# Loading w_in by row blocks, with six open sums for the first two tiles

## The chip, the cores and the metric

The kernel runs on one core of a Trainium2 chip. The metric is the device time of one execution in microseconds. Before the change the median of three runs is 207.99 us (207.76 to 208.26).

## The reference

Two mixers are computed from the same x (2048 rows of 512) and blended by a gate per row. Mixer A is a linear attention with softmax features over 32 heads of 16. Mixer B is a gated MLP with a product over the sequence:

```python
z = gelu(x @ w_in)                        # 512 -> 1376
z1, z2 = z[:, :688], layernorm(z[:, 688:])
g = w_sp @ z2 + b_sp[:, None]             # over the 2048 rows
b = (z1 * g) @ w_out                      # 688 -> 512
gate = sigmoid((x * gate_w).sum(-1, keepdims=True))
out = gate * a + (1 - gate) * b
```

The change touches only how `x @ w_in` and `x * gate_w` are computed for the first 256 of the 2048 rows, and how w_in is loaded.

## The kernel before

The 2048 rows are 16 tiles of 128. The contraction over 512 is cut into four blocks of 128, called dt. `w_in` is kept as four blocks of 128 rows by 1377 columns: 1376 of w_in, and gate_w as column F = 1376, so that a tile's z product also gives the logit of its gate. A tile's z takes three PSUM banks. Even tiles use banks 0 to 2 and odd tiles banks 3 to 5 (`zbank`), so tile 2 can write a bank only when the gelu has read tile 0's values there, and tile 3 follows tile 1 in the same way.

The order on each engine is written out by hand. At the start:

- Loads. The first two tiles of x are loaded as they are (L108 on SP's queue, L109 on ScalarE's). w_in follows (L112): columns 0 to 255 and 256 to 511, each as two blocks on SP and two on ScalarE's queue, then columns 512 to 1023 as two transfers on SP, then, after gate_w (L120, ScalarE's queue), columns 1024 to 1375 of all four blocks in one transfer on SP (L122). Behind that, on SP, come the transposing load of x for tiles 2 and 3 (L123), wv (L124), and the further loads of x, of the attention weights and of w_sp. The compiled program reuses eight DMA semaphores in turn, so that an SP issue can wait for the landing of the transfer eight places before it.
- TensorE. 24 products of a constant (`spin`, L189), which compute nothing that is used, then eight products that transpose x of tiles 0 and 1 (L195). VectorE copies tile 0's result into xT (L204), ScalarE tile 1's (L206). After four more spins come the z products of tiles 0 and 1 (`z_piece`, L180): for columns 0 to 255, then 256 to 511, then 512 to 1023, over the four blocks, tile 0 and tile 1 in turn.
- The gate column. gate_w is transposed by TensorE (L209), and VectorE casts it into column F of w_in (L212). The last z products of a tile are 353 columns wide and contain it.
- `z_post` takes the gelu on ScalarE (L215), the gate's tanh (L222), and the statistics of the layernorm on VectorE (L224, L227). For tile 0 parts of the gelu come earlier, as soon as a bank is complete.

Then tiles 2 to 15 run alike, twelve z products each (four of 512, four of 512, four of 353 columns), and from tile 5 on with the v projection of an older tile (L282) and the folding of the attention weights (L305) between them. The stages behind (features, the product with w_sp at L405, the attention, the output) aren't touched.

Of the kernel before, what the change touches and what calls it, by code (L numbers as in the profile page):

```python
# [19 lines left out]
F = 1376  # L20
FH = 688
HF = FH // 2
NT = S // P
NDT = D // P
CH = 512
# [14 lines left out]
def kernel(  # L40
# [14 lines left out]
    nc = tc.nc  # L55
# [11 lines left out]
    def zbank(t):  # L67
        b = 3 * (t % 2)
        return ps[:, b:b + 3, :].rearrange("p b n -> p (b n)")

    xT = pers.tile([P, NDT, S], BF16, name="xT")
    w_in = pers.tile([P, NDT, F + 1], BF16, name="w_in")
# [30 lines left out]
        out=ident[:], in_=ident[:], pattern=[[-1, P]],  # L103
# [3 lines left out]
    w_in_v = B_w_in.rearrange("(dt p) f -> p dt f", p=P)  # L107
    nc.sync.dma_start(out=xn[:, 0, :], in_=x2[0:P, :])  # L108
    nc.scalar.dma_start(out=xn[:, 1, :], in_=x2[P:2 * P, :])  # L109

    def load_w_in(eng, d0, d1, n0, n1):
        eng.dma_start(out=w_in[:, d0:d1, n0:n1], in_=w_in_v[:, d0:d1, n0:n1])  # L112

    HC = CH // 2
    for n0 in (0, HC):
        load_w_in(nc.sync, 0, 2, n0, n0 + HC)
        load_w_in(nc.scalar, 2, 4, n0, n0 + HC)
    for d0 in (0, 2):
        load_w_in(nc.sync, d0, d0 + 2, CH, 2 * CH)
    nc.scalar.dma_start(out=gw[:], in_=gate_w.rearrange("(dt p) -> dt p", p=P))  # L120
    nc.scalar.activation(out=st[:, 9, 0:1], in_=ones[:, 0:1], func=AF.Gelu_apprx_tanh)
    nc.sync.dma_start(out=w_in[:, :, 2 * CH:F], in_=w_in_v[:, :, 2 * CH:F])  # L122
    nc.sync.dma_start_transpose(out=xT[:, :, 2 * P:CH], in_=x2[2 * P:CH, :])  # L123
    nc.sync.dma_start(  # L124
        out=wv[:, :, :],
        in_=A_wqkv[:, 2 * D:3 * D].rearrange("(dt p) n -> p dt n", p=P),
    )
    for q in range(1, NCH):
        nc.sync.dma_start_transpose(
            out=xT[:, :, q * CH:(q + 1) * CH], in_=x2[q * CH:(q + 1) * CH, :]  # L130
        )
        if q == 1:
            nc.sync.dma_start(
                out=wphiW[:, :, :],
                in_=A_w_phi.rearrange("(g h) e f -> (h e) g f", g=NDT),
# [3 lines left out]
        out=bcolb[:, :, :], in_=B_b_sp.rearrange("(t p) -> t p", p=P)  # L139
# [7 lines left out]
    for t in range(WSLOTS):  # L147
        load_wsp(t)
    nc.sync.dma_start(
        out=w_out[:, 0:NFT - 1, :],  # L150
        in_=B_w_out[0:(NFT - 1) * P, :].rearrange("(ft p) n -> p ft n", p=P),
# [4 lines left out]
        out=w_out[0:last_m, NFT - 1, :], in_=B_w_out[(NFT - 1) * P:FH, :]  # L156
    )
    nc.sync.dma_start(
        out=wo[:, :, :], in_=A_wo.rearrange("(g p) n -> p g n", p=P)
# [4 lines left out]
        out=mask16[:], in_=mask16[:], pattern=[[-16, 8]],  # L164
# [3 lines left out]
        out=mask16[:], in_=mask16[:], pattern=[[16, 8]],  # L168
# [8 lines left out]
    def z_piece(t, n0, n1, d0=0, d1=NDT):  # L177
        zb = zbank(t)
        for dt in range(d0, d1):
            nc.tensor.matmul(  # L180
                zb[:, n0:n1], lhsT=xT[:, dt, t * P:(t + 1) * P], rhs=w_in[:, dt, n0:n1],
                start=(dt == 0), stop=(dt == NDT - 1),
            )

    Z_PIECES = [(0, CH), (CH, 2 * CH), (2 * CH, F + 1)]

    def spin(n):
        for _ in range(n):
            nc.tensor.matmul(  # L189
                ps[:, 5, 0:P], lhsT=ones, rhs=ones, start=True, stop=True  # L190
            )

    def x_transpose(t):
        for dt in range(NDT):
            nc.tensor.matmul(  # L195
                ps[:, 6 + t, dt * P:(dt + 1) * P], lhsT=xn[:, t, dt * P:(dt + 1) * P],
                rhs=ident[:], start=True, stop=True,
            )
# [9 lines left out]
    def gate_column():  # L208
        nc.tensor.matmul(  # L209
            ps[:, 6, 0:NDT], lhsT=gw[:], rhs=ident[0:NDT, 0:NDT], start=True, stop=True  # L210
        )
        nc.vector.tensor_copy(out=w_in[:, :, F], in_=ps[:, 6, 0:NDT])  # L212

    def z_gelu(t, n0, n1):
        nc.scalar.activation(  # L215
            out=zz[:, t, n0:n1], in_=zbank(t)[:, n0:n1], func=AF.Gelu_apprx_tanh
        )

    def z_post(t, done=0):
        zb = zbank(t)  # L220
        z_gelu(t, done, F)
        nc.scalar.activation(out=gth[:, t:t + 1], in_=zb[:, F:F + 1], func=AF.Tanh, scale=0.5)  # L222
        for h in range(2):
            nc.vector.bn_stats(  # L224
                out=stats[:, t, h, :], in_=zz[:, t, FH + h * HF:FH + (h + 1) * HF]
            )
        nc.vector.bn_aggr(out=mv[:, t, :], in_=stats[:, t, :, :].rearrange("p h s -> p (h s)"))  # L227
# [241 lines left out]
    oTpool = ctx.enter_context(tc.tile_pool(name="oTp", bufs=LAG + 2))  # L469

    VLAG = 5
    spin(24)
    x_transpose(0)
    x_transpose(1)
    for d0, d1 in ((0, 1), (1, 2), (2, NDT)):
        x_copy(0, d0, d1)
        x_copy(1, d0, d1)
    spin(4)
    for n0, n1 in ((0, HC), (HC, CH), Z_PIECES[1]):
        for dt in range(NDT):  # L480
            z_piece(0, n0, n1, dt, dt + 1)
            z_piece(1, n0, n1, dt, dt + 1)
        if n1 == CH:
            z_gelu(0, 0, CH)
            gate_column()
    z_gelu(0, *Z_PIECES[1])
    z_piece(0, *Z_PIECES[2])
    z_post(0, done=2 * CH)
    z_piece(1, *Z_PIECES[2])
    z_post(1)  # L490
    build_wphi()
    for t in range(2, NT):
# [96 lines left out]
```

## Time and profile before

| What | us |
|---|---|
| median of three runs | 207.99 |
| the profiled execution | 208.12 |
| its span, first to last instruction | 206.4 |
| TensorE busy | 202.3 |
| VectorE busy | 148.5 |
| ScalarE busy | 82.1 |
| z products (L180), 200 of them | 39.7 |
| product with w_sp (L405), 512 of them | 84.1 |

The busy time of TensorE counts overlapping matmuls once, and an instruction's own duration is longer than the distance to the next one, since they are pipelined. A price per matmul is therefore read from the distance of starts, or from the chain, which lays the pieces end to end. What the DMA queues bring in the first microseconds, by the page:

```profile
w_in<-in_B_w_in_dram SPq DMA_DIRECT2D x2, 256.0 KB, 4.5
...
w_in<-in_B_w_in_dram SPq DMA_DIRECT2D x1, 352.0 KB, 4.9
w_in<-in_B_w_in_dram ACTq DMA_DIRECT2D x2, 128.0 KB, 4.0
w_in<-in_B_w_in_dram SPq DMA_DIRECT2D x2, 128.0 KB, 3.6
```

The columns are the destination and source, the queue, the number of transfers, the size of each (in KiB), and the median time from issue to landing.

### The profile page before, as it was taken

How to read it: one execution, taken by the hardware profiler on the slowest of the kernel's cores; microseconds unless marked ns; L12 is line 12 of the kernel's file. 1: busy time of each engine (PE TensorE's matmuls, PEld its weight loads, DVE VectorE, ACT ScalarE, POOL GpSimd, SP SyncE). 2: the span in 40 equal slices, each digit the busy share in tenths (PEclk: the TensorE clock that was granted, in tenths of full speed). 3: DMA queues.
4: the chain of work that ended last, by engine and by line, in shares of the span. 5: the costliest groups of instructions: out<-in, count | busy, mean ns of one | idle time of the engine just before them, and what ended most of it. 6: DMA issues, size and time to landing. Idle time of an engine off the chain costs nothing.

```text
span 206.4 us, 3685 instructions
## 1 busy us (share of the span) xinstructions
PE 202.3 (98%) x1399; PEld 117.8 (57%) x1399; DVE 148.5 (72%) x304; ACT 82.1 (40%) x145; POOL 49.5 (24%) x46
## 2 busy tenths in 40 slices
PE   8999999999999999999999999999999999999994
PEld 8545555554455666666666667666455555555542
DVE  1049858385887888879898996798989788796500
ACT  4266767675684324250505102222524243341122
POOL 4000000000002353525352543032532252322000
PEclk9999999999999999999999999999999999999999
DMA  5999899997000638463757781145756974566451
GB/s 160 289 178 247 189 170 226 168 192 231 0 3 0 140 65 117 102 112 85 153 126 109 139 174 41 38 91 84 161 131 122 127 176 98 129 141 153 110 110 51
DMA packets 90378, 26.50 MB, mean 128 GB/s; under 512 B 84296, under 2 KB 90360, under 8 KB 90360
## 3 DMA queue, kind: packets, MB, share of 16 engines
q1 hardware_dynamic: 87360, 23.87, 60.2%
q10 hardware_dynamic: 3000, 2.39, 3.8%
q8 instruction: 11, 0.18, 0.4%
q14 instruction: 7, 0.06, 0.1%
HBM read 3.44 MB, written 2.10 MB: 27 GB/s over the span
## 4 chain that ended last, share of the span: by engine, by line
PE 96%; DMA 2%; SPq 0%; ACT 0%; issue 0%
PE ps L405 36%; PE ps L180 18%; PE ps L326 13%; PE ps L448 10%; PE ps L453 7%; PE ps L282 7%; DMA w_in<-in_B_w_in_dram 2%; PE ps L427 2%; PE ps L377 2%; PE ps L305 1%; SPq L112 0%; SPq L108 0%; ACT ob L457 0%; PE ps L209 0%
## 5 line engine op out<-in xcount | busy, mean ns | idle before, releaser
L405 PE MATMUL ps<-zz,wsp 128*128 128x344 bf16 x512 | 84.1, 309 | 0.0
L343 POOL TENSOR_TENSOR w_in<-w_in,rs 128x512 bf16<-128x512 bf16 x28 | 41.3, 1475 | 124.7 <-DVE rs L341 112.4
L405 PEld LDWEIGHTS <-wsp 128*128 128x128 bf16 x512 | 49.9, 98 | 28.1
L334 ACT ACTIVATE w_in<-ps 128x512 bf16<-128x512 f32 x56 | 30.1, 596 | 63.3 <-issue 21.4
L180 PE MATMUL ps<-w_in,xT 128*128 128x512 bf16 (+2 forms) x200 | 39.7, 350 | 0.4 <-DMA w_in<-in_B_w_in_dram 0.4
L339 DVE TENSOR_REDUCE zs<-w_in 128x64 f32<-128x1024 bf16 x28 | 33.8, 1209 | 0.0
L413 DVE SCALAR_TENSOR_TENSOR u<-ps,bcol,zz 128x344 bf16<-128x344 f32 x32 | 18.4, 574 | 18.6 <-PE ps L427 8.3
L180 PEld LDWEIGHTS <-xT 128*128 128x128 bf16 x200 | 19.1, 98 | 18.0 <-issue 0.8
L215 ACT ACTIVATE zz<-ps 128x1376 bf16<-128x1376 f32 (+2 forms) x18 | 21.4, 1190 | 18.6 <-PE ps L180 18.6
L448 PE MATMUL ps<-w_out,uT 128*128 128x512 bf16 (+2 forms) x102 | 23.5, 366 | 0.0
L224 DVE BATCH_NORM_STATS2 stats<-zz 128x6 f32<-128x344 bf16 x32 | 14.8, 505 | 11.1 <-ACT zz L215 11.1
L377 PE MATMUL ps<-vv,w_in 128*128 128x65 bf16 x128 | 21.7, 193 | 0.0
L343 DVE TENSOR_TENSOR w_in<-w_in,rs 128x512 bf16<-128x512 bf16 x28 | 19.4, 693 | 1.0
L341 DVE RECIPROCAL rs<-zs 128x64 f32<-128x64 f32 x32 | 17.7, 553 | 3.2
L457 ACT ACTIVATE ob<-ps 128x512 bf16<-128x512 f32 (+2 forms) x17 | 9.7, 572 | 25.1 <-PE ps L453 19.9
L453 PE MATMUL ps<-wo,oT 128*128 128x512 bf16 (+2 forms) x68 | 16.6, 366 | 0.0
L326 PEld LDWEIGHTS <-xT 128*128 128x128 bf16 x128 | 10.8, 98 | 9.9
L326 PE MATMUL ps<-wq,xT 128*128 128x512 bf16 x64 | 16.4, 379 | 0.0
L326 PE MATMUL ps<-wk,xT 128*128 128x512 bf16 x64 | 16.3, 379 | 0.0
L427 PE MATMUL ps<-kvx,wqkT 128*128 128x68 bf16 x128 | 15.8, 194 | 0.0
L282 PE MATMUL ps<-wv,xT 128*128 128x512 bf16 x64 | 15.6, 379 | 0.0
L448 PEld LDWEIGHTS <-uT 128*128 128x128 bf16 x102 | 9.5, 98 | 10.4
(56 smaller groups left out, 134.3 us busy)
## 6 DMA issues: line engine op xcount, KB each, us to landing
out_dram<-ob ACTq DMA_DIRECT2D x15, 128.0 KB, 2.1
w_out<-in_B_w_out_dram SPq DMA_DIRECT2D x1, 640.0 KB, 4.9
w_in<-in_B_w_in_dram SPq DMA_DIRECT2D x2, 256.0 KB, 4.5
wv<-in_A_wqkv_dram SPq DMA_DIRECT2D x1, 512.0 KB, 5.0
wo<-in_A_wo_dram SPq DMA_DIRECT2D x1, 512.0 KB, 5.3
w_in<-in_B_w_in_dram SPq DMA_DIRECT2D x1, 352.0 KB, 4.9
w_in<-in_B_w_in_dram ACTq DMA_DIRECT2D x2, 128.0 KB, 4.0
w_in<-in_B_w_in_dram SPq DMA_DIRECT2D x2, 128.0 KB, 3.6
```

The lines of the kernel that those rows point to most:

```text
L180: nc.tensor.matmul(zb[:, n0:n1], lhsT=xT[:, dt, t * P:(t + 1) * P], rhs=w_in[:, dt, n0:n1], start=(dt == 0), stop=(dt == NDT - 1),)
L215: nc.scalar.activation(out=zz[:, t, n0:n1], in_=zbank(t)[:, n0:n1], func=AF.Gelu_apprx_tanh)
L282: nc.tensor.matmul(ps[:, b, :], lhsT=xT[:, dt, t * P:(t + 1) * P], rhs=wv[:, dt, :], start=(dt == 0), stop=(dt == NDT - 1),)
L326: nc.tensor.matmul(ps[:, b, :], lhsT=xT[:, dt, t * P:(t + 1) * P], rhs=w[:, dt, :], start=(dt == 0), stop=(dt == NDT - 1),)
L334: nc.scalar.activation(out=e[:, :, a, :], in_=src, func=AF.Exp, scale=sc)
L339: nc.vector.tensor_reduce(out=zs[:], in_=ev, axis=AX.X, op=ALU.add)
L343: eng.tensor_tensor(out=ev[:, sl, :], in0=ev[:, sl, :], in1=rs[:, sl, None].to_broadcast([P, H, DH]), op=ALU.mult,)
L377: nc.tensor.matmul(slots[:, g, 0:HW + 1], lhsT=ek_t[t][:, g, :, :].rearrange("p a n -> p (a n)"), rhs=vv[:, t, g, 0:HW + 1], start=(t == 0 ...
L405: nc.tensor.matmul(ps[:, b, 0:HF], lhsT=wsp[:, tt % WSLOTS, s, :], rhs=zz[:, s, FH + h * HF:FH + (h + 1) * HF], start=(s == 0), stop=(s == ...
L427: nc.tensor.matmul(slots[:, g, 0:QW], lhsT=eT_t[t][:, g, :], rhs=kvx[:, g, :], start=True, stop=True)
L448: nc.tensor.matmul(ps[:, b, n0:n1], lhsT=uT[:, ft, :], rhs=w_out[:, ft, n0:n1], start=(ft == 0), stop=False,)
L453: nc.tensor.matmul(ps[:, b, n0:n1], lhsT=oT[:, g, :], rhs=wo[:, g, n0:n1], start=False, stop=(g == NDT - 1),)
```

## The change

w_in is loaded by blocks of its rows, all 1376 columns at once. Blocks 0 and 1 are each cut in two halves of 688 columns, one on SP's queue and one on ScalarE's; blocks 2 and 3 are one transfer each on SP. There are six transfers of w_in where there were seven.

The z products of tiles 0 and 1 go over dt on the outside: each block feeds six products (512, 512 and 352 columns for each tile) into six sums that stay open in six banks. The column of the gate is taken out of them. Its transpose by TensorE comes after the second block, and eight products of one column follow the last block. All gelus of the two tiles come after them in program order. There are three more spins at the start. Tiles 2 to 15 are as before.

```diff
-    def load_w_in(eng, d0, d1, n0, n1):
-        eng.dma_start(out=w_in[:, d0:d1, n0:n1], in_=w_in_v[:, d0:d1, n0:n1])
-
-    HC = CH // 2
-    for n0 in (0, HC):
-        load_w_in(nc.sync, 0, 2, n0, n0 + HC)
-        load_w_in(nc.scalar, 2, 4, n0, n0 + HC)
-    for d0 in (0, 2):
-        load_w_in(nc.sync, d0, d0 + 2, CH, 2 * CH)
+    def load_w_in(eng, dt, n0, n1):
+        eng.dma_start(out=w_in[:, dt, n0:n1], in_=w_in_v[:, dt, n0:n1])
+
+    for dt in (0, 1):
+        load_w_in(nc.sync, dt, 0, FH)
+        load_w_in(nc.scalar, dt, FH, F)
     nc.scalar.dma_start(out=gw[:], in_=gate_w.rearrange("(dt p) -> dt p", p=P))
     nc.scalar.activation(out=st[:, 9, 0:1], in_=ones[:, 0:1], func=AF.Gelu_apprx_tanh)
-    nc.sync.dma_start(out=w_in[:, :, 2 * CH:F], in_=w_in_v[:, :, 2 * CH:F])
+    for dt in (2, 3):
+        load_w_in(nc.sync, dt, 0, F)
...
-    spin(24)
+    spin(27)
...
-    for n0, n1 in ((0, HC), (HC, CH), Z_PIECES[1]):
-        for dt in range(NDT):
-            z_piece(0, n0, n1, dt, dt + 1)
-            z_piece(1, n0, n1, dt, dt + 1)
-        if n1 == CH:
-            z_gelu(0, 0, CH)
+    FIRST = [(0, CH), (CH, 2 * CH), (2 * CH, F)]
+    for dt in range(NDT):
+        for t in (0, 1):
+            for n0, n1 in FIRST:
+                z_piece(t, n0, n1, dt, dt + 1)
+        if dt == 1:
             gate_column()
-    z_gelu(0, *Z_PIECES[1])
-    z_piece(0, *Z_PIECES[2])
+    for t in (0, 1):
+        z_piece(t, F, F + 1)
+    z_gelu(0, *FIRST[0])
+    z_gelu(0, *FIRST[1])
     z_post(0, done=2 * CH)
-    z_piece(1, *Z_PIECES[2])
     z_post(1)
```

## The prediction

> **What bounds the kernel now.** I read the page's busy shares first, then the chain that ended last, then the first 24 us engine by engine, then the DMA rate stretch by stretch.
>
> ```profile
> PE 202.3 (98%) x1399; PEld 117.8 (57%) x1399; DVE 148.5 (72%) x304; ACT 82.1 (40%) x145; POOL 49.5 (24%) x46
> ...
> PE 96%; DMA 2%; SPq 0%; ACT 0%; issue 0%
> ```
>
> TensorE is busy 98% of the span and is 96% of the chain. So the end moves only if TensorE's work changes or its idle time does. The 2% of DMA in the chain is the one stretch that this edit touches.
>
> ```profile
> 0.83 2.72 PE L189 MATMUL ps<-const-bfloat16-1.0 128*128 128x128 bf16 x24 [0.83 <-PEq L573]
> ...
> 3.38 1.03 PE L195 MATMUL ps<-ident,xn 128*128 128x128 bf16 x8
> ...
> 4.64 1.15 PE L180 MATMUL ps<-w_in,xT 128*128 128x256 bf16 x8
> 6.22 1.05 PE L180 MATMUL ps<-w_in,xT 128*128 128x256 bf16 x8 [0.43 <-DMA w_in<-in_B_w_in_dram]
> ...
> 7.21 0.17 PE L209 MATMUL ps<-ident,gw 4*128 4x4 bf16 x1
> ...
> 7.31 12.57 PE L180 MATMUL ps<-w_in,xT 128*128 128x512 bf16 x64
> ...
> 8.96 0.18 DVE L212 CAST w_in<-ps 128x4 bf16<-128x4 f32 x1 [4.12 <-DMA w_in<-in_B_w_in_dram]
> ...
> 19.72 1.03 PE L282 MATMUL ps<-wv,xT 128*128 128x512 bf16 x4
> ```
>
> The reader should see three things: TensorE waits at 6.22 for the second w_in pieces; the cast of the gate column waits for the last w_in piece and comes at 8.96; and from 7.31 on L180 runs as one block up to 19.72. No wait of TensorE is listed behind 6.22, so whatever the first two tiles gain or lose reaches the end unchanged.
>
> Unit prices come from the chain of the same stretch:
>
> ```profile
> 19.88 0.86 PE ps L282 x4
> 20.75 0.22 PE ps L305 x4
> 20.97 2.33 PE ps L180 x12
> ```
>
> A 512-wide product takes 0.86/4 = 0.216 us, a 128-wide one 0.22/4 = 0.056, and a tile of twelve z products 2.33, which leaves (2.33 - 8 x 0.216)/4 = 0.15 for a 353-wide one. The spins at the start are 128 wide too but stand 0.107 apart (2.72 us for 24), so TensorE runs at half speed there, though the page's clock row prints a full grant; by the starts of the first z products, 0.21 and then 0.11 apart, full speed comes at 4.86. Tile 2 starts four tiles before 19.72: 19.72 - 4 x 2.33 = 10.39. This is the mark to compare.
>
> **The change, part by part** (profiled execution: 208.12 us, a span of 206.4 and 1.7 around it; it lies 0.13 over the median 207.99).
>
> Spins, three added: 3 x 0.107 = 0.32. Before, TensorE stood 0.04 for x to land (3.34), and that goes, so transposes and first z product come 0.28 to 0.31 later: the first z product at 4.95 instead of 4.64. The casts of xT on VectorE and ScalarE move along by 0.31; tile 1's first is then written by about 5.05 and its first product comes at 4.95 + 0.58 = 5.53, so they stay hidden.
>
> z products: 32 become 24 wide ones, the same columns; two tiles cost 2 x 2.33 = 4.66. The 256-wide ones stand 0.109 apart, so halving cost nothing before either.
>
> Gate column's transpose (L209), moved behind the second block: before, it stretched the step from a 256-wide product to the next one from 0.11 to 0.31, so 0.20, and I keep that. Its weights gw lie behind the ACT queue's w_in pieces in both kernels and are wanted at 4.95 + 2.33 = 7.28, about when they are now.
>
> Gate column's products, eight added, one column wide, each with its own 128x128 weights. The trace has no one-column product. Low end: the 68-wide L427 starts 0.03 before its successor, 8 x 0.03 = 0.24. High end: the isolated 4-wide L209 at 0.20, 8 x 0.20 = 1.6. These eight have the weights' shape and no change of shape between, like L427, so I take 0.24 and keep 1.6 as a rival. The 353rd column that they replace is worth 0.4 ns each.
>
> The wait of the cast L212 moves off the path: it is released by the last block and is wanted only at 9.8. Behind it on VectorE stand tile 0's statistics, which follow tile 0's last gelu (about 10.6) and so don't meet it. Before, it cost the step from 512 to 353 wide: 7.31 to 10.39 is 3.08 for 8 x 0.216 + 8 x 0.15 = 2.93, so 0.15.
>
> Sum without a DMA wait: 4.95 + 4.66 + 0.20 + 0.24 = 10.05 for tile 2, 0.34 earlier than 10.39.
>
> Loads. Starts plus time to landing give for the pieces now: 128 KiB each at 4.06 (SP) and 4.34 (ACT), 6.18 (SP) and 6.64 (ACT), then 256 KiB at 7.02 and 7.83, and the last 352 KiB at 8.88. The new blocks are 344 KiB (352 kB) each, with rows of 1376 or 2752 bytes for 512, 1024 and 704. The rates:
>
> ```profile
> 3.50:4.50 1.00, 1.00 (x12) 1.00 (x11) 0.47 (x3) 0.95 (x3) 0.00 (x0) 1.00 0.96 230
> 4.50:5.50 1.00, 1.00 (x11) 0.82 (x9) 0.35 (x2) 0.68 (x3) 0.00 (x0) 1.00 0.90 258
> ...
> 6.50:7.50 1.00, 1.00 (x9) 0.62 (x8) 0.00 (x0) 0.30 (x1) 0.00 (x0) 1.00 1.09 354
> ```
>
> The last column is GB/s: 230 and 258 while the 512-byte rows go, 354 with the longer rows, at much the same busy share of the DMA engines. Early end: 90 kB more than the first pair (4.34) and then 352 kB each at 354 GB/s: 4.6, 5.6, 6.6, 7.6. Late end, today's landings by bytes: 5.13, 6.90, 7.85, 8.88. TensorE wants them at 4.95 (ACT's half 0.22 later), 6.11 (6.33), 7.47 and 8.63. At the early end nothing waits; at the late end only the second block does. Rows are 2.7 to 5.4 times those that were slow, so I stand near the early end and put 0.1 us on the second block.
>
> The Trainium skill ("DMA: Bandwidth & Descriptors", Specifications) says that transfers of 512 B and up already reach line rate, so longer rows would bring nothing; by that rule the late end holds. The trace disagrees so far, 230 against 354 GB/s.
>
> ScalarE: all gelus of the first two tiles now come behind the last block. Tile 0's first can start at 9.05 (its last product begins at 8.63 and takes 0.38), then 0.6, 0.6, 0.46, 0.17 and tile 1's 1.32: done by 12.2 at the latest. Tile 3, which wants tile 1's banks, starts at 10.05 + 2.33 = 12.38. The cover is 0.18 us; if it goes, tile 3 waits by what is missing.
>
> SP: one issue of 0.47 less in front, so the x transpose for tiles 2 and 3 is issued about 0.5 earlier. It landed at 9.85 (4.47 + 5.4), 0.96 behind the last w_in piece; it may not land later than 10.05, which holds even at the late end. The later loads on SP come earlier too.
>
> **Total:** 208.12 - 0.34 + 0.1 = 207.88 for this execution, 207.75 against the median. The 0.1 is the softest term; I forecast 207.7. A measurement here tells a change from none at about 0.2%, 0.42 us; 207.7 is inside.
>
> **The rivals.**
> (a) *Clock opens early.* The old kernel's tile 2 hangs on landings (last one 8.88, cast 9.14, then 8 x 0.15), so it doesn't care when full speed comes; the new one does. With full speed from the transposes on, their 12 matmuls take 0.67 for 1.28, but the first block lands at 4.6, so tile 2 starts at 9.70, 0.69 earlier: 207.3. For it: nothing else would bind. Against: this profile shows 4.86.
> (b) *Clock opens late*, 1 us: the first products run at half speed, 0.5 back: 10.55, so 0.16 later: 208.15.
> The Trainium skill ("TensorE: Matmul & The Clock Gate", Part 1) puts the opening some 4 us into sustained activity, give or take 0.5. The trace agrees, 4.86 - 0.83 = 4.03; that other executions differ isn't shown here.
> (c) *Row blocks land as bytes do today.* The second block's second half at 6.90 instead of 6.33 costs 0.57: 10.62, 208.2; if both halves land together the loss is 0.79: 10.84, 208.4. For it: the ACT pieces always landed 0.27 to 0.46 behind SP's. Against: the rates above.
> (d) *The slower side: one-column products cost what the isolated L209 does.* Tile 2 at 4.95 + 4.66 + 0.20 + 1.6 = 11.41, so 1.02 later: 209.0. It turns slower from 0.24/8 + 0.34/8 = 0.07 us each, and beyond 0.2% from 0.125. For it: eight sums into two columns, the weights changed each time. Against: L427 and L377 at 0.03.
>
> **Chances.** Forecast 0.42, (a) 0.24, (b) 0.07, (c) 0.17, (d) 0.10. The forecast gives 0.08 of its part to faster, as 207.57 is close; (a) is faster; (c) is split 0.08 within and 0.09 beyond (208.41), (b) 0.05 and 0.02, (d) 0.01 and 0.09. Faster 0.32, within 0.34 + 0.08 + 0.05 + 0.01 = 0.48, slower 0.20. Low end of the range: (a) with another 0.1, 207.2. High end: (c) in its worse form with 0.1, 208.5. Left out are (d) and the edge of (a) and (b).
>
> **What would show it.** First L180 product at 4.95; no wait of TensorE within the 24, or one short one at 6.1 to 6.3; L212's cast about 8 with nobody behind it; eight narrow L178 products within 0.3 us; tile 2 at 10.0 to 10.2; full use of TensorE after that. Wrong: a long wait for w_in inside the 24 (c), a stretch above 0.6 us for the narrow products (d), first products 0.43 apart (b), a wait of tile 3 for ScalarE, or of tile 2 for the x transpose.

## The result, and the profile after

The changed kernel takes 208.66 us (median of 19 runs, 207.80 to 209.52) against 207.97 (19 runs, 207.67 to 208.36) on the same chip: a ratio of 1.0034, 95% interval 1.0021 to 1.0047. It is slower, by 0.7 us, and its single runs lie 1.7 us apart where those of the old kernel lie 0.7 apart. The profiled execution took 208.91, a span of 207.2.

The page of the changed kernel, the lines that answer to the first ones shown before:

```profile
PE 202.5 (98%) x1402; PEld 117.7 (57%) x1402; DVE 148.6 (72%) x304; ACT 81.9 (40%) x145; POOL 49.5 (24%) x46
...
PE 95%; DMA 3%; ACTq 0%; ACT 0%; issue 0%
```

TensorE's busy time is 0.2 us more, while the span is 0.8 longer: TensorE stands longer, and the chain puts it down to DMA, 3% where it was 2%. The timeline of the first microseconds tells where:

```profile
0.84 3.04 PE L187 MATMUL ps<-const-bfloat16-1.0 128*128 128x128 bf16 x27 [0.84 <-PEq L572]
...
4.95 1.55 PE L178 MATMUL ps<-w_in,xT 128*128 128x512 bf16 x7
...
7.43 1.12 PE L178 MATMUL ps<-w_in,xT 128*128 128x512 bf16 x5 [0.93 <-DMA w_in<-in_B_w_in_dram]
...
8.48 0.17 PE L207 MATMUL ps<-ident,gw 4*128 4x4 bf16 x1
...
8.59 8.69 PE L178 MATMUL ps<-w_in,xT 128*128 128x512 bf16 x50
8.69 0.18 DVE L210 CAST w_in<-ps 128x4 bf16<-128x4 f32 x1 [3.53 <-PE ps L207]
10.19 1.50 ACT L213 ACTIVATE zz<-ps 128x512 bf16<-128x512 f32 x3 [4.70 <-PE ps L178]
```

Seven products run from 4.95: the six of block 0 and the first of block 1. The eighth needs the columns of block 1 that ScalarE's queue loads, and starts at 7.43. The seventh started at 6.13, so the step that should take 0.22 took 1.31: a loss of 1.09 us (the 0.93 in brackets counts from the modelled end of the seventh). Behind it TensorE runs without a stop. The landing of the two halves of block 1, from the view of the tile w_in in the stretch in which they are issued (SP's and ScalarE's at 1.72 and 1.73; shortest, median and longest time to landing):

```profile
DMA to landing us min/median/max: 4.2/4.9/5.7
```

SP's half lands at 5.93, ScalarE's at 7.39. They were issued together and are the same size. Block 2 (7.58) and block 3 (8.45) are then in time.

```profile
20.64 0.86 PE ps L280 x4
```

This row of the chain answers to the one at 19.88 before. All is later by 0.76, so tile 2 starts at 10.39 + 0.76 = 11.15.

The rate at which the data came (us; then busy time of TensorE, weight loads, VectorE, ScalarE, GpSimd; granted clock, DMA share, GB/s):

```profile
3.50:4.50 1.00, 1.00 (x12) 1.00 (x11) 0.16 (x1) 0.81 (x2) 0.00 (x0) 1.00 1.11 376
4.50:5.50 1.00, 1.00 (x10) 0.76 (x8) 0.66 (x3) 0.72 (x3) 0.00 (x0) 1.00 0.99 331
5.50:6.50 1.00, 1.00 (x6) 0.39 (x4) 0.00 (x0) 0.00 (x0) 0.00 (x0) 1.00 1.03 407
6.50:7.50 1.00, 0.07 (x2) 0.07 (x1) 0.00 (x0) 0.00 (x0) 0.00 (x0) 1.00 1.93 213
```

331 to 407 GB/s from 3.5 to 6.5, where the old kernel had 230 to 312 in the trace of the prediction (275 to 336 in a second one, below). The bytes came faster than in the first, and yet ScalarE's half of block 1, wanted at 6.34, landed at 7.39, only 0.19 before block 2.

The trace's DMA records, one for each row (a contiguous piece of a transfer, which goes to one partition), suggest how. They don't name the DMA engine, so what follows is put together from their times. In the trace the semaphore of such a transfer is counted up 16 times. For ScalarE's half of block 1, 14 of the 16 counts are there by 5.43, the 15th at 5.94 and the last, which is the landing, at 7.39. So most of the 16 DMA engines were done early, and one was behind: two rows took 0.73 and 0.42 us, where a row of 1376 bytes takes 0.059. When that engine came to ScalarE's half, SP's queue had block 2 waiting on it, and the rows alternated:

```
ScalarE's queue, rows of 1376 B, start: 6.22  6.38  6.55  6.72  6.88 us; the end mark (4 bytes) 7.04
step: 0.16 to 0.17 us = 0.059 (its row) + 0.109 (a row of 2752 B of block 2 on SP's queue)
```

After the end mark at 7.04 comes the last count at 7.39. So, as far as the times tell, one DMA engine of 16 set the landing.

### The profile page after: what moved, and what is told of

It reads as the page before. It is cut to its first block, busy times and chain, and to the rows that moved or that the text cites. A ratio compares the mean times of both kernels' runs of the same rounds, so it can differ in the third digit from the quotient of the medians.

```text
span 207.2 us, 3688 instructions
## 1 busy us (share of the span) xinstructions
PE 202.5 (98%) x1402; PEld 117.7 (57%) x1402; DVE 148.6 (72%) x304; ACT 81.9 (40%) x145; POOL 49.5 (24%) x46
## 4 chain that ended last, share of the span: by engine, by line
PE 95%; DMA 3%; ACTq 0%; ACT 0%; issue 0%
PE ps L403 36%; PE ps L178 18%; PE ps L324 13%; PE ps L446 10%; PE ps L451 7%; PE ps L280 7%; DMA w_in<-in_B_w_in_dram 3%; PE ps L425 2%; PE ps L375 2%; PE ps L303 1%; ACTq L112 0%; ACTq L109 0%; ACT ob L455 0%; PE ps L207 0%
## 5 line engine op out<-in xcount | busy, mean ns | idle before, releaser
L178 PE MATMUL ps<-w_in,xT 128*128 128x512 bf16 (+3 forms) x200 | 39.7, 349 | 0.9 <-DMA w_in<-in_B_w_in_dram 0.9
L178 PEld LDWEIGHTS <-xT 128*128 128x128 bf16 x200 | 18.5, 98 | 18.9 <-issue 1.2
L324 PEld LDWEIGHTS <-xT 128*128 128x128 bf16 x128 | 10.8, 98 | 9.9
```

The source lines that it names most:

```text
L178: nc.tensor.matmul(zb[:, n0:n1], lhsT=xT[:, dt, t * P:(t + 1) * P], rhs=w_in[:, dt, n0:n1], start=(dt == 0), stop=(dt == NDT - 1),)
L324: nc.tensor.matmul(ps[:, b, :], lhsT=xT[:, dt, t * P:(t + 1) * P], rhs=w[:, dt, :], start=(dt == 0), stop=(dt == NDT - 1),)
```

## The experiments

Theory A: ScalarE's half of block 1 is late because of the long rows of block 2 that alternate with it. Theory B: block 1 would be late in any queue. A third theory, C, came out of the first four traces. Ratios are to the old kernel, run on the same chip; the chip isn't the same for all experiments.

**Block 1 in one transfer on SP, behind its half of block 0.**

```diff
-    for dt in (0, 1):
-        load_w_in(nc.sync, dt, 0, FH)
-        load_w_in(nc.scalar, dt, FH, F)
+    load_w_in(nc.sync, 0, 0, FH)
+    load_w_in(nc.scalar, 0, FH, F)
+    load_w_in(nc.sync, 1, 0, F)
```

> Block 1 goes as one transfer on SP's queue; ScalarE's queue keeps x, half of block 0 and gate_w. In the changed kernel the only wait inside the 24 z products is for ScalarE's half of block 1, landing at 7.39; SP's half landed at 5.93. Theory A (the half is late because on a DMA engine that fell behind its rows alternate with SP's rows of block 2, twice as long): in one queue block 1 can't be overtaken by block 2, lands at about 6.0 to 6.5, the wait shrinks from 1.1 us to at most 0.2, tile 2 starts at 10.05 to 10.3 instead of 11.15, and the time falls by 0.8 to 1.0 us to 207.6 to 207.9. Theory B (the bytes or a stalled DMA engine make block 1 late in whatever queue it is): block 1 lands at 6.9 or later, a wait of 0.6 to 1.1 us stays, 208.3 to 208.7.

208.54 against 207.78, 1.0033 (1.0020 to 1.0045). Block 1 landed at 6.78, between what the two theories had put. Nothing of the loss went away: as put, theory A is wrong. Putting block 1 in front of block 2 in one queue doesn't help as long as its own rows are long. The wait in this trace was only 0.2 us, though, as A had put and B had not; another 0.48 went to a cause that neither theory had (theory C below).

**Block 2 in two halves of columns.**

```diff
-    for dt in (2, 3):
-        load_w_in(nc.sync, dt, 0, F)
+    load_w_in(nc.sync, 2, 0, FH)
+    load_w_in(nc.sync, 2, FH, F)
+    load_w_in(nc.sync, 3, 0, F)
```

> Block 2 goes on SP's queue as two halves of 688 columns, so that the rows that alternate with ScalarE's half of block 1 are 1376 bytes long instead of 2752. Theory A: on an engine that is behind, a pair of rows takes 2 x 0.059 = 0.12 us instead of 0.16, over 8 pairs 0.35 us less; the half of block 1 lands about 0.35 earlier and the time is about 208.3 (half of the gap to the kernel with block 1 on SP at most). Theory B: row length of what runs beside it doesn't matter, 208.6 to 208.8.

207.70 against 207.78, 1.0002 (0.9988 to 1.0016). Block 1 landed at 5.50 and 5.68 and TensorE didn't wait. That is more than A had expected.

**Only the gate column moved, the old loads kept.**

```diff
-    z_piece(0, *Z_PIECES[2])
-    z_post(0, done=2 * CH)
-    z_piece(1, *Z_PIECES[2])
+    for t in (0, 1):
+        z_piece(t, 2 * CH, F)
+    for t in (0, 1):
+        z_piece(t, F, F + 1)
+    z_post(0, done=2 * CH)
```

> The old kernel with its old loads; only the gate column is taken out of the 353-wide products of tiles 0 and 1 and put behind them as eight products of one column. Theory A: this part is worth -0.15 (the wait for the cast goes) and +0.2 (8 x 0.025), though the last w_in piece's landing at 8.88 still bounds the 352-wide products: between -0.1 and +0.1 us, 207.9 to 208.1. A rival that puts the loss of the changed kernel into the narrow products or the later gelus expects 208.4 or more.

208.10, 1.0012 (0.9998 to 1.0026), not told from no change. The expectation was put against 207.99; the old kernel took 207.78 on this chip, so the rival's loss of 0.4 us would be a ratio of 1.0020, inside the interval: this run doesn't rule it out. The trace of the changed kernel does, in which eight narrow products take 0.20 us and tile 3 doesn't wait for the gelus. In the trace of this run the 352-wide products start at 9.34, 0.57 after the last piece of w_in had landed (8.77), so there the loads didn't set the start of tile 2.

**24 spins in the changed kernel** (`spin(27)` back to `spin(24)`).

> The changed kernel with 24 spins instead of 27. Theory A and B: the first z product comes 0.28 us earlier, but the wait for block 1 takes it back, so no change against the changed kernel, 208.5 to 208.8. Rival (the three spins are what the change lost): 0.3 us less, 208.35, with the wait for block 1 no longer than before.

207.96, 1.0013 (0.9997 to 1.0029). Neither theory had this: with the loads of the changed kernel, more than half of the loss was gone by the medians, though the interval reaches into that of the changed kernel. Its trace has block 1 at 5.86 and 6.04 and no wait, with block 2 in long rows: they don't delay block 1 in every execution. An earlier start of the z products explains 0.3 us at most; the rest stays unexplained.

These traces brought up something that the page doesn't show. The trace's clock record, which begins when TensorE gets its full speed, begins at another time in each: 4.86 (old kernel), 4.97 (changed), 5.92, 4.78, 6.60 and 4.81 us. The page prints a full clock from the start of the span in all of them. Theory C: the changed kernel, bound by TensorE from 4.95 on, pays half of every microsecond by which full speed is late; the old one spends that time waiting for loads. It was put to the test with the next four.

**The changed kernel unaltered, beside three variants.**

> The changed kernel, unaltered, beside three variants on one chip, for the comparisons and for a second trace. Theory A (queue): again a wait of about 1 us for the second block, and 208.6. Theory C (new: full speed of TensorE comes at another time in each execution; it came at 4.86, 4.97, 5.92, 4.78, 6.60 and 4.81 us in the six traces so far, and the changed kernel, which is bound by TensorE from 4.95 on, loses half of what it comes later, while the old one waits for loads in that time): the median is the same 208.5 to 208.7, but the second trace shows less wait where full speed came later, and the tile-2 start is 10.05 plus half of (full speed - 4.95) plus any wait.

208.98 against 207.94, 1.0052 (1.0031 to 1.0073). The timeline of this second trace of the changed kernel:

```profile
4.72 1.32 PE L178 MATMUL ps<-w_in,xT 128*128 128x512 bf16 x6
6.51 0.38 PE L178 MATMUL ps<-w_in,xT 128*128 128x512 bf16 x1 [0.47 <-DMA w_in<-in_B_w_in_dram]
7.74 1.12 PE L178 MATMUL ps<-w_in,xT 128*128 128x512 bf16 x4 [0.85 <-DMA w_in<-in_B_w_in_dram]
```

Full speed came early here (4.43), and TensorE waited for both halves of block 1, landing at 6.47 and 7.70. ScalarE's half ended on rows 0.16 us apart again.

**Block 2 in halves, again, and with 24 spins.**

> Block 2 in two halves on SP's queue, again, now beside the changed kernel on the same chip. Theory A: 0.4 us or more below the changed kernel (the first time 207.70 against 207.78 for the old one). Theory C alone: the row length of block 2 does nothing, the same as the changed kernel within 0.2 us, and the first result was the chip or luck.

> Block 2 in two halves and 24 spins. Theory A: at most 0.3 us below the kernel with 27 spins, as the second block still lands at 5.7 to 6.0 and is wanted at 5.8. Theory C: the z products start 0.3 us earlier, and half-speed products are done while TensorE would be spinning, so 0.15 to 0.3 us below the one with 27 spins whatever the loads do. Both: about 207.4, which would be under the old kernel.

208.03, 1.0004 (0.9993 to 1.0014), and 207.71, 0.9995 (0.9983 to 1.0006). So on one chip the short rows take 0.95 us off the changed kernel, with intervals that don't overlap, and bring it to the old one. The three spins are worth 0.3 us by the medians, within the intervals.

**36 spins in place of 4 in front of the z products.**

```diff
-    spin(4)
+    spin(36)
```

> The changed kernel with 36 spins instead of 4 between the copies of xT and the z products, so that every block has landed before it is wanted and only TensorE's speed sets the start of tile 2. Theory C: the time is 209.2 to 209.4 when full speed comes at 4.87 and half a microsecond more for each microsecond later, so the single runs spread over more than 1 us, up to 210.8, with a median about 210. A and B, with full speed always near 4.9: all runs within 0.3 us of 209.3.

209.87, 1.0089 (1.0072 to 1.0107), runs from 209.26 to 210.30. TensorE has no wait for a load in its trace:

```profile
4.53 2.83 PE L187 MATMUL ps<-const-bfloat16-1.0 128*128 128x128 bf16 x36
7.19 2.50 PE L178 MATMUL ps<-w_in,xT 128*128 128x512 bf16 x11
9.62 0.17 PE L207 MATMUL ps<-ident,gw 4*128 4x4 bf16 x1
```

The 36 spins start at 4.53 and end at 7.19, 0.074 each on average, between 0.107 and 0.056, so full speed came in the middle: their starts fall from 0.107 to 0.058 apart at about 5.74 (this trace has no clock record). The five runs spread over 1.04 us, though no load is waited for; but the 26 runs of the old kernel on this chip spread over 1.06, so the spread alone doesn't single out the clock. The median, 209.87, is 0.5 to 0.7 above the 209.2 to 209.4 of full speed at 4.87 and near the 210 that theory C had put; A and B had put 209.3. Theory C holds here, and the starts of the spins show the change of speed directly. The trace also gives the pure price of the stretch: from the first z product to tile 2, 12.28 - 7.19 = 5.09 us at full speed (four blocks, the transpose and the narrow products).

**A control for the short rows: two transfers for block 2, cut by partitions.**

```diff
+    for p0 in (0, P // 2):
+        nc.sync.dma_start(
+            out=w_in[p0:p0 + P // 2, 2, 0:F], in_=w_in_v[p0:p0 + P // 2, 2, 0:F]
+        )
```

> A control for the short rows of block 2: block 2 again in two transfers on SP, issued at the same times as the two column halves, but cut by partitions, so that its rows keep 2752 bytes. Theory A (row length of what alternates with ScalarE's half of block 1): as the changed kernel, block 1 complete at 7.2 to 7.7, ratio to the old kernel 1.003 to 1.005. Rival D (two smaller transfers, the second issued 1.1 us later, let block 1 through): as with short rows, block 1 complete at 5.7 to 6.6, ratio 1.000 to 1.0005.

208.55, 1.0030 (1.0021 to 1.0038): as the changed kernel. Same number of transfers, same order, long rows, and the loss is back. The two halves of block 1 landed at 6.57 and 6.75 in its trace, later than with short rows (5.50 and 5.68; 5.95 and 6.60) and earlier than I had put. So by the run times the rows of block 2 decide, not the number of transfers or when they are issued. The trace doesn't show the path, as TensorE waits for no load in it:

```profile
4.95 3.23 PE L181 MATMUL ps<-w_in,xT 128*128 128x512 bf16 x12
```

What this execution lost, it lost to a late full speed (6.42).

**One queue, short rows** (block 1 on SP in two column halves, block 2 too).

> Block 1 on SP's queue in two halves of 688 columns, block 2 too. With block 1 as one transfer of long rows on SP it landed at 6.78 and the ratio was 1.0033. If short rows as such make block 1 land in time: 6.0 to 6.4 and a ratio of 1.000 to 1.001. If what counts is that two queues feed the DMA engines at once (a stalled packet of one leaves the engine to the other): block 1 complete at 6.6 or later, ratio 1.002 or more, as with long rows.

207.98, 1.0000 (0.9989 to 1.0011), block 1 complete at 5.81. One queue does as well as two, if the rows are short. In its trace TensorE waits for no load, and yet:

```profile
4.95 3.34 PE L180 MATMUL ps<-w_in,xT 128*128 128x512 bf16 x12
8.22 0.17 PE L209 MATMUL ps<-ident,gw 4*128 4x4 bf16 x1
```

Twelve products and the step to the transpose take 8.22 - 4.95 = 3.27, where full speed needs 2 x 1.16 + 0.1 = 2.42. The 0.85 more is half of the 1.69 by which full speed (6.64) came after the first product. This kernel's runs fall in two groups, 207.54 to 207.79 and 208.17 to 208.56.

**One queue, block 1 short, block 2 long.**

> Block 1 on SP in two halves of short rows, block 2 behind it on the same queue in one transfer of long rows. Theory A (the harm is the alternation with the other queue): block 2's rows can't get between block 1's, so block 1 is complete by 5.8 to 6.4, as with short rows everywhere, ratio 0.999 to 1.001. Rival E (long rows anywhere among the first three blocks slow the DMA engines down): block 1 or block 2 late by 0.5 us or more, ratio 1.002 to 1.005.

208.39, 1.0016 (1.0002 to 1.0029), between the two expectations; its interval touches both that of the changed kernel and that of short rows everywhere. In its trace, where full speed came early (3.53), block 1 landed at 6.29 and 6.74 and cost 0.77 and 0.24 us by the distances of starts. So long rows behind a short block in the same queue, where nothing can alternate with another queue, may cost something too. But with short rows everywhere (the next run) block 1 landed at 6.19 and 6.66, hardly earlier. This stays open.

**Attempts at a faster kernel.**

> Block 1 and block 2 in short rows on SP, 24 spins instead of 27. If TensorE bounds the stretch, as theory C says where the loads are in time: 0.15 to 0.3 us under the one with 27 spins (ratio 1.000), so 0.9987 to 0.9993. If the landings bound it: 1.000.

207.82, 0.9995 (0.9985 to 1.0006). In its trace the first z product starts at 4.40, which takes full speed for the last spins, and TensorE then waited for block 1 (6.19 and 6.66): when the clock is early the landings bound the stretch.

> An attempt to beat both kernels: short rows for block 2, 24 spins, gate_w loaded by GpSimd's queue and transposed by TensorE before the z products, in place of two spins. The transpose's 0.2 us leave the stretch that TensorE bounds: against the kernel with short rows and 24 spins (ratio 0.9995) 0.2 us less, a ratio of 0.9985 if TensorE bounds the stretch; unchanged if the landings or the clock do.

208.60, 1.0042 (1.0022 to 1.0062), with runs up to 210.4. gate_w landed at 5.26 and TensorE stood for it, here in the trace (the 0.58 counts from a modelled end):

```profile
5.30 0.18 PE L209 MATMUL ps<-ident,gw 4*128 4x4 bf16 x1 [0.58 <-DMA gw<-in_gate_w_dram]
5.42 7.74 PE L180 MATMUL ps<-w_in,xT 128*128 128x512 bf16 x34
```

In that execution (210.4 us) full speed came at 10.04 only. ScalarE's half of block 1 landed at 7.28, although block 2 went in short rows; at half speed TensorE didn't wait for it.

> Short rows for block 2, 24 spins, and gate_w on ScalarE's queue between its halves of blocks 0 and 1, with TensorE's transpose of it in place of two spins in front of the z products. gate_w should land by 4.5, so that TensorE doesn't stand as it did with GpSimd's load (5.26). If TensorE bounds the stretch: 0.2 us under the kernel with 24 spins (ratio 0.9995), so 0.998 to 0.999. If gate_w lands later than 4.6, or the landings of block 1 bound the stretch: no gain or a loss, 0.9995 or more.

207.91, 1.0004 (0.9988 to 1.0020): no gain.

```profile
4.99 0.16 PE L209 MATMUL ps<-ident,gw 4*128 4x4 bf16 x1 [0.39 <-DVE xT L204]
5.09 7.20 PE L180 MATMUL ps<-w_in,xT 128*128 128x512 bf16 x41
```

This time gate_w isn't what TensorE stands for: the transpose writes the bank from which VectorE is still copying xT. What was saved later was lost here.

**The old kernel once more.**

> The old kernel, for another trace. Theory C: wherever full speed comes between 4.4 and about 6.5, tile 2 starts at 10.3 to 10.6, since the last w_in piece (8.9) and the cast bound it.

One run, 207.85. Full speed came at 5.51, 0.65 later than in its first trace, and tile 2 started at 10.15, 0.24 earlier, as the last piece of w_in landed at 8.65 instead of 8.88. It follows the landing (1.51 behind it in both traces), not the clock, but the 10.3 to 10.6 were too narrow. How far this goes is seen above, in the run with the gate column moved: with full speed at 6.60 its products, in the order of the old kernel up to there, came later than the landing.

## Why the prediction was wrong

The forecast was 207.7, within 0.2% of the old kernel, with a range of 207.2 to 208.5; the time is 208.66, above it. By its steps:

- Spins: right. The first z product was put at 4.95 and came at 4.95; in the other traces with 27 spins and this order it came between 4.39 and 4.96, early where full speed was early.
- Wide products, transpose and narrow products: right. 4.66 + 0.20 + 0.24 were 5.10; without a wait it is 5.09. The narrow products start 0.025 us apart in the trace, so rival (d) is out.
- The cast L210 holds nobody up, the gelus don't hold up tile 3, and the x transpose lands at 9.98, before tile 2 wants it: as put, though 0.13 later than before and not earlier. Tile 2 at the forecast 10.05 would have had 0.07 of cover.
- Loads: this is the term that failed. I put "0.1 us on the second block"; it cost 1.09 in the first trace and 1.64 in the second (both halves late). The step that failed is "Rows are 2.7 to 5.4 times those that were slow, so I stand near the early end". I took the rate for the landing. Even my late end, 6.90, the landing by bytes of rival (c), lay below the 7.39 and 7.70 measured; that rival had the wait in the right place, at 0.57 to 0.79 us. By the run times the rows that I counted as a gain were what cost: with rows of 1376 bytes for block 2 the ratio is 1.0002 and 1.0004, with 2752 bytes 1.0034, 1.0052 and, in two transfers, 1.0030, all with 27 spins. In one queue: 1.0033 with both blocks long, 1.0016 with block 2 long, 1.0000 with both short.
- The rates, on which that step stood, didn't show what I read in them. Of the 258 kB that moved from 4.5 to 5.5 in the old kernel, 163 were in rows of 1024 bytes already; its second trace has 275 and 336 GB/s where the first has 230 and 258; and the kernel with block 1 whole on SP has 239 and 250 there, with rows of 1376 and 2752 bytes. So 230 against 354 GB/s was no measure of the row length. I also overlooked that at the late end the first block, 5.13 against 4.95, would have waited too; it doesn't change that sum, as the second block's landing sets it.
- The clock: rivals (a) and (b) had the mechanism, and "it doesn't care when full speed comes; the new one does" is what was found. The sum, though, took the 4.86 of one trace as the rule, and I gave the early side 0.24 and the late side 0.07. With short rows no wait is left, the sum without a wait says -0.34, and the kernel measures as the old one: by the traces the clock takes most of the difference. It cost 0.65 and 0.85 in the traces where it came at 6.25 and 6.64, and 0.23 on average over the eight traces with 27 spins and the changed kernel's order (first z product against 4.95, plus the half-speed loss).

The Trainium skill ("TensorE: Matmul & The Clock Gate", Part 1) has the opening some 4 us into sustained activity, give or take 0.5. The first trace agreed; of all 14 traces that have a clock record and kept TensorE busy up to it, 7 agree and 7 don't: counted from TensorE's first product at 0.83 or 0.84, it took from 2.7 (one queue, block 2 long) to 5.8 us (one queue, short rows).

How far the two terms carry, trace by trace (us): first z product + 5.09 + half of what full speed came later + waits for loads, against the start of tile 2 that the trace has.

| kernel | first z | full speed | half-speed loss | waits | sum | tile 2 |
|---|---|---|---|---|---|---|
| changed | 4.95 | 4.97 | 0.01 | 1.09 | 11.14 | 11.15 |
| changed, second trace | 4.72 | 4.43 | 0 | 1.64 | 11.45 | 11.46 |
| block 1 long on SP | 4.96 | 5.92 | 0.48 | 0.2 | 10.73 | 10.76 |
| block 2 short | 4.88 | 4.78 | 0 | 0 | 9.97 | 9.98 |
| block 2 short, again | 4.95 | 6.25 | 0.65 | 0 | 10.69 | 10.70 |
| block 2 long, two transfers | 4.95 | 6.42 | 0.74 | 0 | 10.78 | 10.78 |
| one queue, short | 4.95 | 6.64 | 0.85 | 0 | 10.89 | 10.89 |

The two work against each other in one execution: when full speed comes late, TensorE reaches block 1 later and waits less (0.2 in the third row) or finds it landed (the sixth row has long rows and no wait). That two things can each delay a run would explain why the runs of the changed kernel scatter more than those of the old one, where tile 2 follows the last landing in both traces; no run tests this by itself.

What is shown: that the wait for block 1 is the loss in both traces of the changed kernel; that with 27 spins the row length of block 2 decides the run times (the control with two long transfers); and that the clock moves this stretch by itself (the spins in front of the z products, and the table). Seen in the traces of the changed kernel only, and not proved by an experiment of its own: that the harm comes by rows alternating on an engine that is behind. The landings of single traces don't settle it. With block 1 on two queues it was complete between 6.04 and 7.70 in five traces with block 2 in long rows, and between 5.68 and 7.28 in five with short ones. The two outliers, 6.04 (24 spins) and 7.28 (gate_w on GpSimd's queue), are from kernels with another change besides. The run with block 2 long in one queue falls between, and why 24 spins with long rows lost so little stays open.

No version was found that is faster than the old kernel beyond the uncertainty; the best two, both at 0.9995, aren't told from it.

## What to carry to other kernels

A block that others wait for lands when the last of its DMA engines is done with it (here the last of 16 counts came 1.45 us behind the 15th): judge a load by its landing and by what shares its engines, not by the rate. Here shorter rows for what was queued behind it were worth 0.95 us on one chip; by which path is open, so try it rather than count on it. Before a start-up stretch is moved from being bound by loads to being bound by TensorE, ask when full speed comes; if that varies between executions, the old waits were hiding it, and one profile can't price it.

## What had not been expected of the hardware

- Full speed of TensorE came between 3.53 and 6.64 us in nine traces with the same 27 spins from 0.84 on (eight by the clock record, one by the starts of the spins). After a stand of 0.58 us in the start (gate_w on GpSimd's queue) it came at 10.04 in one execution.
- The page's clock row doesn't show this; the distance of like products does (0.107 and 0.056 for 128 columns).
- With more than 330 GB/s moving, a single transfer of 172 KiB took 5.7 us to land beside its twin's 4.2: 15 of the 16 counts of its semaphore were there by 5.94, the last at 7.39.
- A load of 1 KiB on GpSimd's queue, issued at 1.44, landed at 5.26.
